# A fused retention and two-FFN kernel: early loads at once, w3 loaded ahead, integer adds in the weights' conversion, a separate pool for late raw words

## The chip, the cores and the metric

The kernel runs on one core of a Trainium2 chip. The metric is the device time of one execution in microseconds (us). TensorE is called PE here, VectorE DVE, ScalarE ACT, GpSimd POOL; SP is the engine whose queue issues most of the transfers.

## The reference, cut to what matters

```python
# attention: batch 4, heads 8, sequence 768, head size 64
for t in range(S):
    state = gamma[None, :, None, None] * state + np.einsum('bhd,bhe->bhde', k[:, :, t], v[:, :, t])
    y[:, :, t] = scale * np.einsum('bhd,bhde->bhe', q[:, :, t], state)
x = np.ascontiguousarray(attn_out.transpose(0, 2, 1, 3)).reshape(B * S, H * D)   # 3072 x 512
# first FFN: w_in 512 x 2048, w_out 2048 x 512
h = x @ w_in
g = np.where(h >= 1, h, np.where(h <= -1, 0.0, (h + 1) ** 2 / 4.0))
x = g @ w_out
# second FFN: w1, w2 512 x 1024, w3 1024 x 1024, w_out 1024 x 512
a = x @ w1
b = x @ w2
return ((a * b) @ w3) @ w_out
```

The inputs q, k and v are float32. The weights are drawn in float64, so each is a pair of 32-bit words in memory; the kernel makes a float32 of the pair on the chip.

## The kernel before, in words

**Retention** runs over 24 chunks of 128 tokens (six to a batch). A chunk `g` is three *pieces*: piece 0 multiplies kT and q (PE L348) and masks the result into `a_t` (DVE L391); piece 1 adds k and v to the state (PE L358, DVE L400 to L406); piece 2 makes the chunk's output (PE L372), whose high part is cast to `xh` (ACT L412) and whose rest is `xl` (DVE L417). Ahead of its pieces a chunk's q and v are scaled on POOL (`scale_chunk`, L315 and L316) into `q_t` and `vp`. q and kT have two buffers each, v and k one each. Four chunks make one tile of 512 tokens; six tiles share two buffers of `xh` and `xl`.

**First FFN.** A *slot* `n` is one tile and one of 16 blocks of 128 hidden features, 96 slots in all; `SLOTS` gives the order: features 0 to 7 of tile 0 (slots 0 to 7), then of tile 1, then 8 to 15 of both, then tiles 2 to 5 whole. A slot is 12 matmuls into `hps` (three passes over high and low halves, `mm3` at L102 to L104), the clipped square (ACT L461 and L462, DVE L463), and the product with `w_out` into `y1acc`: another 12 matmuls, or, for slots below `PLAIN`, 4 in plain float32 (L513).

**Conversion.** A weight pair goes through a *job*: raw words are loaded by SP (`load_job`, L127 and L131), ACT takes the absolute value of the high words (L168), and DVE shifts, masks and scales in five steps (L184 to L203), then adds the two parts (L215, L231 or L242). Early jobs hold 1024 words of each partition, later ones 512. `win` jobs and `wo` jobs alternate, and the raw words of all share two buffers, so that each kind has one. After slot `PLAIN` a second pool of conversion buffers takes the rest of `w_in` and `w_out`, and then the weights of the second FFN, which are converted and put back to memory (*spilled*). Between the steps of a job other work is set by a planner, which keeps estimates of when each engine is free (`now`) and lets a job's next step go if it fits in front of the next step of a slot.

**Second FFN.** w3 and the last weight are folded first: the *w3 stage*, 16 groups `u` of 12 matmuls into `w3acc`. Its w3 groups are fetched from memory (`fetch`, L275), each into one of two buffers, two groups ahead; in between the operands for the next stage are prepared. Then come 24 *units* into `bank_a`, `bank_b` and `bank_c` and the output products (`oacc`).

```python
def chunk_ahead(a):
    g, part = divmod(a, PIECES)
    if a < TILE_PIECES:
        if part == 0:
            if g:
                load_qk(g + 1)
            scale_chunk(g + 1)
        elif part == 1:
            load_k(g + 1)
            load_v(g + 2)
...
            load_w3(u + 1)
            if u + 2 < 2 * NF2:
                fetch(("w3", u + 2), spill[("w3", u + 2)])
            emit_w3o(u)
```

Of the kernel before, what the change touches and what calls it, by code (L numbers as in the profile page):

```python
# [16 lines left out]
P = 128  # L17
# [20 lines left out]
PLAIN = 11  # L38
SINGLE = 1
LATE = 5  # L40
# [9 lines left out]
def retention_then_two_ffns(  # L50
# [22 lines left out]
    ps_h = ctx.enter_context(tc.tile_pool(name="ps_h", bufs=2, space=bass.MemoryType.PSUM))  # L73
    ps_a = tc.tile_pool(name="ps_a", bufs=1, space=bass.MemoryType.PSUM)
    pairs_psum = ctx.enter_context(ExitStack())
    ps_a = pairs_psum.enter_context(ps_a)
    dram = ctx.enter_context(tc.tile_pool(name="dram", bufs=1, space=bass.MemoryType.DRAM))
    retention, splits, conversion = (ctx.enter_context(ExitStack()) for _ in range(3))
# [13 lines left out]
    state = const.tile([P, NP, D], F32, name="state")  # L92
    cpool = conversion.enter_context(tc.tile_pool(name="cpool0", bufs=2))
# [20 lines left out]

    def load_job(j):
        src, n, key, _ = j
        if key not in loaded:
            loaded.add(key)
            raw = cpool.tile([P, 2 * n], U32, tag="raw", name="raw")
            if key[0] == "win":  # L120
# [3 lines left out]
                for h in range(2):  # L124
                    for c in range(2):
                        for i in range(n // 512):
                            nc.sync.dma_start(  # L127
                                out=to[64 * c:64 * c + 64, i, h], in_=of[64 * h:64 * h + 64, i, :, c]
                            )
# [32 lines left out]
    magnitudes = {}  # L162

    def magnitude(job):
# [4 lines left out]
        magnitudes[key] = u  # L169
        now["conv"] = ready[("raw", key)] + 1.1  # L170

    def converter():

        while jobs:
            job = jobs.popleft()
            _, n, key, done = job
            if key not in magnitudes:
                magnitude(job)
            now["dve"] = max(now["dve"], now["conv"])
            raw, u = raws.pop(key), magnitudes.pop(key)  # L180
            lo, hi = raw[:, 0::2], raw[:, 1::2]
            w = cpool.tile([P, n], F32, tag="wf", name="w_f")
            uf, wu = u.bitcast(F32), w.bitcast(U32)
# [22 lines left out]
            yield 0.2 + n / 960  # L206
            if jobs:
                magnitude(jobs[0])
            if len(jobs) > 1:
                load_job(jobs[1])  # L210
            yield from done(w, uf)

    def done_win(f):
        def done(w, u):
            nc.vector.tensor_tensor(out=w, in0=w, in1=u, op=ALU.add)  # L215
# [10 lines left out]
    def done_wo(f):  # L226
        def done(w, u):
            for i in range(w.shape[-1] // 512):
# [11 lines left out]
    def done_spill(key):  # L240
        def done(w, u):
            nc.vector.tensor_tensor(out=w, in0=w, in1=u, op=ALU.add)  # L242
# [29 lines left out]
    def fetch(key, src):  # L272
        one = key[0] in ("wo2", "w3")
# [37 lines left out]
    def scale_chunk(g):  # L311
        if g >= NG:
# [4 lines left out]
            out=vp[g % 2],  # L317
# [16 lines left out]
    def piece_mm(a):  # L334
# [4 lines left out]
        q_t, kb, vb = ch[g], kp[g % 2], vp[g % 2]  # L339
        if part == 1 and c == NCH - 1:  # L340
            return
        ps = ps_a.tile([P, 2, 512], F32, tag="pa", name="pa")
        if part == 0:

            for p in range(NP):
                for h in range(2):
                    r = slice(64 * h, 64 * h + 64)
                    nc.tensor.matmul(  # L348
                        out=ps[:, h, p * C:(p + 1) * C], lhsT=kb[r, p, :], rhs=q_t[r, p, :],
# [3 lines left out]
        elif part == 1:  # L353

            for p in range(NP):
                for h in range(2):
# [3 lines left out]
                        lhsT=kt[g][:, d0:d0 + D], rhs=vb[:, 2 * p + h, :],  # L360
# [3 lines left out]
        else:  # L364


            for own in (False, True) if c else (True,):
                for j in range(NP // 2):
                    for h in range(2):
                        for e in range(2):  # L370
# [3 lines left out]
                                lhsT=vb[:, 2 * p + h, :] if own else sbd[r, p, :],  # L374
# [7 lines left out]
    def piece_ew(a):  # L382
# [6 lines left out]
        if part == 0:  # L389
            a_t = att.tile([P, 2, NP, C], F32, tag="a", name="a_t", bufs=1)  # L390
# [28 lines left out]
    def chunk_ahead(a):  # L419

        g, part = divmod(a, PIECES)
        if a < TILE_PIECES:
            if part == 0:
                if g:
                    load_qk(g + 1)
                scale_chunk(g + 1)
            elif part == 1:
                load_k(g + 1)
                load_v(g + 2)
        elif part == 0:  # L430
# [304 lines left out]
    with tc.manual_schedule():  # L735
# [6 lines left out]
        for at_, (kind, w, f, done) in enumerate(order):  # L742
# [7 lines left out]
        nc.sync.dma_start(out=decay, in_=c_decay)  # L750
        load_qk(0)
        load_v(0)
        nc.sync.dma_start(out=small, in_=c_small)
        scale_chunk(0)
        load_k(0)
        for h in range(2):
            r = slice(64 * h, 64 * h + 64)
            nc.sync.dma_start(out=block[r], in_=c_block[r, :, 64 * h:64 * h + 64])
        load_qk(1)
        now["dma"] = 9.0  # L760
        load_job(jobs[0])
        load_v(1)


        early = [jobs[1]]
        for a in range(TILE_PIECES):
            piece_mm(a)
            chunk_ahead(a)
            if a == 2:
                load_job(early.pop(0))  # L770
            piece_ew(a)
# [4 lines left out]
        for n in range(-1, NA):  # L776
# [11 lines left out]
            mine = [todo.popleft() for _ in range(mine) if todo]  # L788
# [211 lines left out]
```

## Time and profile before

| | us |
|---|---|
| median of three runs | 1108.78 (1108.28 to 1109.03) |
| profiled execution, whole | 1105.77 |
| its span (first to last instruction) | 1104.0 |
| PE busy | 1050.3 (95%), granted clock 0.985 of 2.4 GHz |
| DVE busy | 698.7 (63%) |
| ACT busy | 433.9 (39%) |
| POOL busy | 71.5 (6%) |
| moved by DMA | 166.03 MB, 150 GB/s on average |

The profiled execution is one run. The 1.77 us between its span and its whole time lie around the instructions, and it is 3.0 below the median.

### The profile page before, as it was taken

What the parts mean: (1) busy time and instruction counts of PE and PEld (TensorE: products, weight loads), DVE (VectorE), ACT (ScalarE), POOL (GpSimd) and SP (SyncE); (2) the same over time, 40 slices, a digit from 0 to 9 for tenths busy, and PEclk for the clock granted to TensorE, in tenths of its full rate; (3) what the DMA queues carried; (4) which work ended last, traced back from release to release, by engine and by line L of the source; (5) the groups of instructions that cost most, each with busy time, mean ns of one, the idle gap of its engine ahead of it and who ended that gap; (6) DMA issues with size and microseconds to landing.
All of it is one profiled execution on the core that took longest, in us unless ns stands there. A gap on an engine that the chain in (4) does not pass through costs nothing.

```text
span 1104.0 us, 14147 instructions
## 1 busy us (share of the span) xinstructions
PE 1050.3 (95%) x5444; PEld 828.7 (75%) x5444; DVE 698.7 (63%) x1130; ACT 433.9 (39%) x763; POOL 71.5 (6%) x67
## 2 busy tenths in 40 slices
PE   4789999899999999999999998689999999999998
PEld 3555578677777777777788886478888888888886
DVE  4798888688888878877835774553445334623340
ACT  1223355344444445454435664432333223412220
POOL 2212000011110100000000010000000000000000
PEclk9789999999999999999999999899999999999999
DMA  6545225254443544354303665554544345523412
GB/s 208 181 154 181 77 96 183 85 172 173 164 152 124 170 136 153 124 173 142 115 2 132 248 239 196 185 200 172 187 166 143 131 176 172 189 105 134 167 34 77
DMA packets 64116, 166.03 MB, mean 150 GB/s; under 512 B 7600, under 2 KB 15920, under 8 KB 59312
## 3 DMA queue, kind: packets, MB, share of 16 engines
q1 hardware_dynamic: 61744, 150.44, 40.1%
q0 software_dynamic: 2304, 14.68, 3.7%
q8 instruction: 43, 0.70, 0.2%
q14 instruction: 25, 0.20, 0.1%
HBM read 125.24 MB, written 39.85 MB: 150 GB/s over the span
## 4 chain that ended last, share of the span: by engine, by line
PE 84%; DVE 6%; DMA 5%; ACT 2%; SPq 1%; issue 1%; POOL 1%; ACTq 0%; POOLq 0%; DVEq 0%
PE bank_a L673 12%; PE hps L103 8%; PE y1acc L102 8%; PE hps L102 8%; PE hps L104 8%; PE y1acc L103 7%; PE y1acc L104 7%; PE bank_b L673 6%; PE oacc L718 4%; PE oacc L720 4%; PE oacc L719 4%; PE bank_c L673 3%; PE pa L372 3%; DMA f<-sp_w 2%; PE y1acc L513 2%; PE pa L348 2%
## 5 line engine op out<-in xcount | busy, mean ns | idle before, releaser
L102 PE MATMUL hps<-xh,win 128*128 128x512 f32 x384 | 154.7, 403 | 6.3 <-ACT win L98 5.0
L103 PE MATMUL hps<-xh,win 128*128 128x512 f32 x384 | 151.7, 395 | 0.5 <-DVE win L99 0.5
L104 PE MATMUL hps<-xl,win 128*128 128x512 f32 x384 | 150.8, 393 | 0.4 <-DVE xl L417 0.4
L673 PE MATMUL bank_a<-yop,unit 128*128 128x512 f32 x576 | 145.7, 389 | 0.0
L102 PE MATMUL y1acc<-gh,wo_s 128*128 128x512 f32 x340 | 139.0, 409 | 4.9 <-ACT wo_s L98 4.9
L461 ACT ACTIVATE r<-hps 128x512 f32<-128x512 f32 x96 | 57.3, 597 | 218.3 <-PE hps L104 218.3
L103 PE MATMUL y1acc<-gh,wo_s 128*128 128x512 f32 x340 | 134.2, 395 | 0.5 <-DVE wo_s L99 0.5
L104 PE MATMUL y1acc<-gl,wo_s 128*128 128x512 f32 x340 | 133.6, 393 | 0.0
L463 DVE SCALAR_TENSOR_TENSOR r<-hps,r 128x512 f32<-128x512 f32 x96 | 66.3, 691 | 101.2 <-ACT r L462 100.7
L673 PEld LDWEIGHTS bank_a<-yop,unit 128*128 128x128 f32 x576 | 108.1, 188 | 22.5
L699 DVE TENSOR_TENSOR c<-bank_b,c 128x512 f32<-128x512 f32 x24 | 16.6, 692 | 131.5 <-PE bank_b L673 131.5
L102 PEld LDWEIGHTS hps<-xh,win 128*128 128x128 f32 x384 | 72.6, 189 | 25.2 <-ACT win L98 5.7
L103 PEld LDWEIGHTS hps<-xh,win 128*128 128x128 f32 x384 | 72.6, 189 | 18.6 <-DVE win L99 1.6
L104 PEld LDWEIGHTS hps<-xl,win 128*128 128x128 f32 x384 | 72.7, 189 | 17.0 <-DVE xl L417 1.3
L102 PEld LDWEIGHTS y1acc<-gh,wo_s 128*128 128x128 f32 x340 | 64.1, 189 | 23.7 <-ACT wo_s L98 5.7
L104 PEld LDWEIGHTS y1acc<-gl,wo_s 128*128 128x128 f32 x340 | 64.1, 189 | 14.5
L103 PEld LDWEIGHTS y1acc<-gh,wo_s 128*128 128x128 f32 x340 | 64.2, 189 | 13.9 <-DVE wo_s L99 1.6
L474 ACT CAST gh<-r 128x512 fp32r<-128x512 f32 x85 | 52.9, 622 | 52.6 <-DVE r L463 52.6
L673 PE MATMUL bank_b<-yop,unit 128*128 128x512 f32 x288 | 73.1, 389 | 0.0
L475 DVE TENSOR_TENSOR gl<-r,gh 128x512 fp32r<-128x512 f32 x85 | 60.6, 713 | 14.9 <-ACT gh L474 13.8
L99 DVE TENSOR_TENSOR wo_s<-wo_f,wo_s 128x512 fp32r<-128x512 f32 x85 | 61.9, 728 | 1.9 <-ACT wo_s L98 1.9
L315 POOL TENSOR_TENSOR q_t<-q_t,decay 128x512 f32<-128x512 f32 x23 | 32.6, 1416 | 465.4 <-DMA q_t<-in_qT_dram 438.0
(152 smaller groups left out, 1716.6 us busy)
## 6 DMA issues: line engine op xcount, KB each, us to landing
unit<-wab_d SPq DMA_DIRECT2D x24, 1024.0 KB, 4.8
unit<-wab_d SPq DMA_DIRECT2D x24, 768.0 KB, 4.3
raw<-in_w_in_dram SPq DMA_DIRECT2D x64, 128.0 KB, 3.0
raw<-in_w_dram SPq DMA_DIRECT2D x16, 512.0 KB, 4.0
raw<-in_w3t_dram SPq DMA_DIRECT2D x16, 512.0 KB, 3.8
wab_d<-four POOLq DMA_DIRECT2D x8, 1024.0 KB, 5.2
raw<-in_w_out_dram SPq DMA_DIRECT2D x14, 512.0 KB, 3.6
q_t<-in_qT_dram SPq DMA_DIRECT2D x24, 256.0 KB, 4.4
```

The source lines that it names most:

```text
L99: nc.vector.tensor_tensor(out=lo, in0=src, in1=hi, op=ALU.subtract)
L102: nc.tensor.matmul(out=ps, lhsT=lh, rhs=rh, start=first, stop=False)
L103: nc.tensor.matmul(out=ps, lhsT=ll, rhs=rh, start=False, stop=False)
L104: nc.tensor.matmul(out=ps, lhsT=lh, rhs=rl, start=False, stop=last)
L461: nc.scalar.activation(out=r, in_=hps[n], func=AF.Relu, bias=0.5, scale=0.5)
L463: nc.vector.scalar_tensor_tensor(out=r, in0=hps.pop(n), scalar=1.0, in1=r, op0=ALU.max, op1=ALU.min)
L474: nc.scalar.copy(out=gh, in_=gs[n])
L475: nc.vector.tensor_tensor(out=gl, in0=gs[n], in1=gh, op=ALU.subtract)
L673: nc.tensor.matmul(out=ps, lhsT=x, rhs=z, start=first and kb + k == 0, stop=kb == 1 and k == 2, skip_group_check=True,)
L718: nc.tensor.matmul(out=ps, lhsT=lh, rhs=wh, start=(f == 0), stop=False)
L719: nc.tensor.matmul(out=ps, lhsT=lh, rhs=wl, start=False, stop=False)
L720: nc.tensor.matmul(out=ps, lhsT=ll, rhs=wh, start=False, stop=(f == NF2 - 1))
```

## The change

1. The sixteen loads of q, kT, v and k of the first four chunks go out at once on SP, into tiles of the pool that weights use later. The constants and the raw words of the first two `win` jobs go out on ACT's queue. The first tile's pieces follow a written order, `EARLY_ORDER`, with two PSUM buffers of their own.
2. A job's low words go through ACT (Relu with a scale, converted to integers), and DVE adds them as integers to the shifted and masked high words; the sign is joined in the step that writes to the destination. Per job DVE has two TENSOR_SCALAR, one integer add and one join per destination; before it had three TENSOR_SCALAR, two SCALAR_TENSOR_TENSOR and the adds.
3. `PLAIN` is 9, it was 11; `LATE`, the number of `win` and `wo` jobs that are cut in halves of 512, is 7, it was 5.
4. Raw words of late jobs have a pool of their own (`rpool`, two buffers), and the first two are loaded four slots before `PLAIN`.
5. w3 is fetched in the last eight slots, into eight tiles of two groups each (`fetch_w3`), not in the w3 stage.

```diff
-PLAIN = 11
+PLAIN = 9
+EARLY_ORDER = [(0, 0), (0, 1), (1, 0), (3, 0), (1, 1), (3, 1), (2, 0), (4, 0), (6, 0), (2, 1), (4, 1), (6, 1)]
+EARLY_ORDER += [(5, 0), (7, 0), (9, 0), (5, 1), (7, 1), (9, 1), (8, 0), (10, 0), (8, 1), (10, 1), (11, 0), (11, 1)]
-LATE = 5
+LATE = 7
...
-            raw = cpool.tile([P, 2 * n], U32, tag="raw", name="raw")
+            pool = rpool if key in late_keys else cpool
+            raw = pool.tile([P, 2 * n], U32, tag="raw", name="raw")
+            queue = nc.scalar if key in first_keys else nc.sync
...
+        r = cpool.tile([P, n], U32, tag="r", name="r")
+        nc.scalar.activation(out=r, in_=raws[key][:, 0::2], func=AF.Relu, scale=2.0 ** -29)
...
-            nc.vector.scalar_tensor_tensor(
-                out=wu, in0=hi, scalar=0xC0000000, in1=u,
-                op0=ALU.bitwise_and, op1=ALU.bitwise_or,
-            )
-            yield 0.2 + n / 960
-            nc.vector.tensor_scalar(
-                out=u, in0=wu, scalar1=0xFF800000, scalar2=None, op0=ALU.bitwise_and
-            )
-            yield 0.2 + n / 1920
-            nc.vector.scalar_tensor_tensor(
-                out=uf, in0=lo, scalar=2.0 ** -52, in1=uf, op0=ALU.mult, op1=ALU.mult
-            )
+            nc.vector.tensor_tensor(out=u, in0=u, in1=r, op=ALU.add)
...
+    def join(out, hi, u):
+        nc.vector.scalar_tensor_tensor(
+            out=out.bitcast(U32), in0=hi, scalar=0xC0000000, in1=u,
+            op0=ALU.bitwise_and, op1=ALU.bitwise_or,
+        )
...
-                nc.vector.tensor_tensor(
-                    out=t, in0=w[:, c0:c0 + 512], in1=u[:, c0:c0 + 512], op=ALU.add
-                )
+                join(t, hi[:, c0:c0 + 512], u[:, c0:c0 + 512])
...
+    def load_early():
+        for g in range(EARLY):
+            qk = wpool.tile([P, 2, 512], F32, tag="w", name="qk_e")
+            vk = wpool.tile([P, 2, 512], F32, tag="w", name="vk_e")
...
+            nc.sync.dma_start(out=ch[g], in_=qT[g])
+            nc.sync.dma_start(out=kb[g], in_=kT[g])
...
+            nc.sync.dma_start(out=vt[g], in_=v[g])
...
+            nc.sync.dma_start(out=kt[g], in_=k[g])
...
+    def fetch_w3(u):
+        t = late.tile([P, 2, 512], F32, tag="wc", name="w3f", bufs=NF2)
+        for i in range(2):
+            nc.sync.dma_start(out=t[:, i, :], in_=spill[("w3", u + i)])
+            arrived[("w3", u + i)] = t[:, i, :]
...
+        load_early()
         load_job(jobs[0])
-        load_v(1)
...
+        load_job(jobs[1])
+        load_qk(EARLY)
+        load_v(EARLY)
+        load_k(EARLY)
+        for g in range(EARLY + 1):
+            scale_chunk(g)
+        load_v(EARLY + 1)
+        for a, ew in EARLY_ORDER:
+            (piece_ew if ew else piece_mm)(a)
...
+            if n == PLAIN - 4:
+                for j in later[:2]:
+                    load_job(j)
...
+                if f >= NF2:
+                    fetch_w3(2 * (f - NF2))
...
-            if u + 2 < 2 * NF2:
-                fetch(("w3", u + 2), spill[("w3", u + 2)])
```

On SP, the loads from chunk 1 to the first `wo` job of before (`in_w_in` is a `win` job's raw words, `in_w_out` a `wo` job's):

```order
L291 DMA q_t<-in_qT_dram 128x512
L292 DMA kp_91<-in_kT_dram 128x512
L127 DMA raw<-in_w_in_dram 64x2x256 x4
L300 DMA v_t<-in_v_dram 128x512
L307 DMA k_t<-in_k_dram 128x512
L300 DMA v_t<-in_v_dram 128x512
L127 DMA raw<-in_w_in_dram 64x2x256 x4
L291 DMA q_t<-in_qT_dram 128x512
L292 DMA kp_90<-in_kT_dram 128x512
L307 DMA k_t<-in_k_dram 128x512
L300 DMA v_t<-in_v_dram 128x512
L131 DMA raw<-in_w_out_dram 128x2048
```

And in the changed program, from the loads of chunk 3 (`qk_e`, `vk_e`) on:

```order
L307 DMA qk_e<-in_qT_dram 128x512
L308 DMA qk_e<-in_kT_dram 128x512
L311 DMA vk_e<-in_v_dram 128x512
L313 DMA vk_e<-in_k_dram 128x512
L320 DMA q_t<-in_qT_dram 128x512
L321 DMA kp_87<-in_kT_dram 128x512
L329 DMA v_t<-in_v_dram 128x512
L337 DMA k_t<-in_k_dram 128x512
L329 DMA v_t<-in_v_dram 128x512
L141 DMA raw<-in_w_out_dram 128x2048
L320 DMA q_t<-in_qT_dram 128x512
L321 DMA kp_88<-in_kT_dram 128x512
```

The `win` loads are gone from this queue, and the first `wo` load stands behind all loads of chunks 0 to 4 and the second `v_t`, the v of chunk 5, which has the buffer of chunk 4's v.

On ACT, the rows around slots 0 and 1 of before (`u<-raw` is the absolute value, `r<-hps` and `r<-r` a slot's activation):

```order
L168 ACTIVATE u<-raw 128x1024
L461 ACTIVATE r<-hps 128x512
L462 ACTIVATE r<-r 128x512
L461 ACTIVATE r<-hps 128x512
L462 ACTIVATE r<-r 128x512
L168 ACTIVATE u<-raw 128x1024
L98 CAST win<-w_f 128x512 x2
```

And in the changed program:

```order
L179 ACTIVATE u<-raw 128x1024
L181 ACTIVATE r<-raw 128x1024
L490 ACTIVATE r<-hps 128x512
L491 ACTIVATE r<-r 128x512
L103 CAST win<-u 128x512
L179 ACTIVATE u<-raw 128x1024
L181 ACTIVATE r<-raw 128x1024
L490 ACTIVATE r<-hps 128x512
L491 ACTIVATE r<-r 128x512
```

A job now has two rows on ACT ahead of the slot's activation, the second (`r<-raw`) with the low words.

## Rows read from the trace of the kernel before

**Rows 1.** Windows by stage: length; busy us (instructions) of PE, PEld, DVE, ACT, POOL; clock, DMA share, GB/s.

```profile
0.00:42.98 42.98, 22.05 (x241) 17.97 (x241) 21.95 (x34) 7.20 (x11) 10.01 (x13) 0.84 0.66 207
42.98:114.90 71.92, 64.40 (x377) 39.63 (x377) 64.24 (x74) 24.25 (x34) 12.64 (x9) 0.95 0.47 154
...
204.00:224.00 20.00, 14.15 (x77) 10.46 (x76) 13.04 (x19) 6.38 (x11) 2.72 (x2) 0.91 0.31 102
224.00:674.26 450.26, 449.40 (x2574) 358.41 (x2572) 344.99 (x596) 220.15 (x396) 41.30 (x38) 1.00 0.44 150
674.26:739.87 65.61, 51.79 (x193) 38.98 (x194) 35.70 (x68) 25.88 (x52) 2.13 (x4) 0.92 0.64 227
739.87:1104.00 364.13, 359.80 (x1584) 296.80 (x1583) 146.71 (x227) 105.86 (x186) 0.00 (x0) 1.00 0.41 140
2.00:12.00 10.00, 4.93 (x48) 4.36 (x48) 2.34 (x3) 0.02 (x1) 2.30 (x2) 1.00 0.98 287
600.00:650.00 50.00, 50.00 (x223) 41.40 (x222) 39.12 (x87) 34.12 (x76) 5.51 (x10) 1.00 0.63 229
```

**Rows 2.** Timeline of PE, first matmuls of slots 0, 2, 8: start, us, [idle before, releaser].

```profile
42.98 0.50 PE L102 MATMUL hps<-xh,win 128*128 128x512 f32 x1 [0.69 <-ACT xh L412]
...
58.15 0.50 PE L102 MATMUL hps<-xh,win 128*128 128x512 f32 x1 [0.58 <-ACT win L98]
...
114.90 0.50 PE L102 MATMUL hps<-xh,win 128*128 128x512 f32 x1 [0.69 <-ACT xh L412]
```

**Rows 3.** The chain that ended last: start, us, engine and line.

```profile
118.67 3.43 PE y1acc L513 x8
...
187.42 1.09 PE pa L348 x16
...
200.56 1.62 PE pa L372 x32
...
207.73 0.59 ACT xh L412
...
212.65 0.62 ACT wo_s L98
...
684.58 6.61 DMA f<-sp_w
...
696.85 7.31 DMA f<-sp_w
...
748.02 2.72 PE bank_a L673 x12
```

**Rows 4.** Groups by shape: count, busy us, mean ns of one, idle before.

```profile
L194 DVE SCALAR_TENSOR_TENSOR w_f<-raw,u 128x1024 uint32<-128x1024 uint32 x10 | 12.2, 1225 | 0.3
L199 DVE TENSOR_SCALAR u<-w_f 128x1024 uint32<-128x1024 uint32 x10 | 6.9, 690 | 0.2
L231 DVE TENSOR_TENSOR wo_f<-w_f,u 128x512 f32<-128x512 f32 x16 | 14.4, 918 | 0.3
L391 DVE TENSOR_TENSOR a_t<-pa,small 128x1024 f32<-128x1024 f32 x24 | 29.2, 1215 | 4.6 <-PE pa L348 4.6
L463 DVE SCALAR_TENSOR_TENSOR r<-hps,r 128x512 f32<-128x512 f32 x96 | 66.3, 691 | 101.2 <-ACT r L462 100.7
L462 ACT ACTIVATE r<-r 128x512 f32<-128x512 f32 x96 | 60.6, 631 | 3.0
L168 ACT ACTIVATE u<-raw 128x1024 f32<-128x1024 f32 x10 | 11.5, 1155 | 9.5 <-DMA raw<-in_w_out_dram 6.8 <-DMA raw<-in_w_in_dram 1.7 <-DMA k_t<-in_k_dram 1.0
L316 POOL TENSOR_TENSOR vp<-v_t,small 128x512 f32<-128x512 f32 x24 | 30.9, 1288 | 8.0 <-DMA small<-in_c_small_dram 5.6 <-DMA v_t<-in_v_dram 2.4
```

**Rows 5.** DMA issues: KB each, median us from issue to landing.

```profile
raw<-in_w_out_dram SPq DMA_DIRECT2D x5, 1024.0 KB, 5.0
raw<-in_w_dram SPq DMA_DIRECT2D x16, 512.0 KB, 4.0
```

**Rows 6.** Waits of PE over the span: us, times, longest.

```profile
PE w3acc L102 <- ACT w3s L98: 10.9, 5, 5.0
```

More of the change, by code (lines that the diff above doesn't have):

```diff
@@ L72, in retention_then_two_ffns @@
     ps_acc = ctx.enter_context(tc.tile_pool(name="ps_acc", bufs=4, space=bass.MemoryType.PSUM))
[L73 to L76, printed above, removed]
+    early_psum, pairs_psum = (ctx.enter_context(ExitStack()) for _ in range(2))
+    ps_a = early_psum.enter_context(
+        tc.tile_pool(name="ps_e", bufs=2, space=bass.MemoryType.PSUM)
+    )
+    ps_h = None
     dram = ctx.enter_context(tc.tile_pool(name="dram", bufs=1, space=bass.MemoryType.DRAM))
[L78 removed]
+    retention, raw_late, splits, conversion = (ctx.enter_context(ExitStack()) for _ in range(4))
     const = retention.enter_context(tc.tile_pool(name="const", bufs=1))
@@ L113, in retention_then_two_ffns @@
     loaded = set()
+    late_keys = set()
+    first_keys = (("win", 0), ("win", 1))
     def load_job(j):
@@ L160, in dma, with tail @@
         return now["dma"] + 1.9
-    magnitudes = {}
-    def magnitude(job):
+    tails = {}
+    def tail(job):
         load_job(job)
@@ L176, in converter @@
             _, n, key, done = job
-            if key not in magnitudes:
-                magnitude(job)
+            if key not in tails:
+                tail(job)
             now["dve"] = max(now["dve"], now["conv"])
[L180 to L183, printed above, removed]
+            raw, (u, r) = raws.pop(key), tails.pop(key)
+            hi = raw[:, 1::2]
+            uf = u.bitcast(F32)
             nc.vector.tensor_scalar(
@@ L226, in done_wo, with done @@
     def done_wo(f):
-        def done(w, u):
-            for i in range(w.shape[-1] // 512):
+        def done(hi, u):
+            for i in range(u.shape[-1] // 512):
                 t = wpool.tile([P, 512], F32, tag="wo", name="wo_f")
                 c0 = i * 512
-                nc.vector.tensor_tensor(
-                    out=t, in0=w[:, c0:c0 + 512], in1=u[:, c0:c0 + 512], op=ALU.add
-                )
+                join(t, hi[:, c0:c0 + 512], u[:, c0:c0 + 512])
                 wo[f + i] = t
@@ L240, in done_spill, with done @@
     def done_spill(key):
-        def done(w, u):
-            nc.vector.tensor_tensor(out=w, in0=w, in1=u, op=ALU.add)
+        def done(hi, u):
+            w = cpool.tile([P, 512], F32, tag="wf", name="w_f", bufs=3)
+            join(w, hi, u)
             d = dram.tile([P, 512], F32, name=f"sp_{key[0]}_{key[1]}")
@@ L316, in scale_chunk @@
         nc.gpsimd.tensor_tensor(
-            out=vp[g % 2],
+            out=vb[g],
             in0=v_t,
@@ L338, in piece_mm @@
         c = g % NCH
-        q_t, kb, vb = ch[g], kp[g % 2], vp[g % 2]
+        q_t, k_, v_ = ch[g], kb[g], vb[g]
         if part == 1 and c == NCH - 1:
             return
-        ps = ps_a.tile([P, 2, 512], F32, tag="pa", name="pa")
+        if g < EARLY and part == 1:
+            ps = ps_acc.tile([P, 1, 512], F32, tag="acc", name="pa")
+        else:
+            ps = ps_a.tile([P, 2, 512], F32, tag="pa", name="pa")
         if part == 0:
@@ L389, in piece_ew @@
         if part == 0:
-            a_t = att.tile([P, 2, NP, C], F32, tag="a", name="a_t", bufs=1)
+            if g < EARLY:
+                a_t = wpool.tile([P, 2, 512], F32, tag="w", name="a_e")
+                a_t = a_t.rearrange("p h (a t) -> p h a t", a=NP)
+            else:
+                a_t = att.tile([P, 2, NP, C], F32, tag="a", name="a_t", bufs=1)
             nc.vector.tensor_tensor(
@@ L421, in chunk_ahead @@
         g, part = divmod(a, PIECES)
[L422 to L430, printed above, removed]
+        if part == 0:
             load_k(g)
@@ L748, in retention_then_two_ffns @@
                 (jobs if at_ < SINGLE else later).append(one)
[L750 to L755, printed above, removed]
+        late_keys.update(j[2] for j in later)
+        nc.scalar.dma_start(out=decay, in_=c_decay)
+        nc.scalar.dma_start(out=small, in_=c_small)
         for h in range(2):
             r = slice(64 * h, 64 * h + 64)
-            nc.sync.dma_start(out=block[r], in_=c_block[r, :, 64 * h:64 * h + 64])
-        load_qk(1)
-        now["dma"] = 9.0
+            nc.scalar.dma_start(out=block[r], in_=c_block[r, :, 64 * h:64 * h + 64])
+        load_early()
         load_job(jobs[0])
-        load_v(1)
[L765 to L771, printed above, removed]
+        load_job(jobs[1])
[7 more added lines that the diff above has]
+            (piece_ew if ew else piece_mm)(a)
+        early_psum.close()
+        ps_h = ctx.enter_context(tc.tile_pool(name="ps_h", bufs=2, space=bass.MemoryType.PSUM))
+        ps_a = pairs_psum.enter_context(
+            tc.tile_pool(name="ps_a", bufs=1, space=bass.MemoryType.PSUM)
+        )
         todo = deque(range(TILE_PIECES, NSTEP))
@@ L806, in retention_then_two_ffns @@
                     jobs.append((w3t[j][:, hf * 512:(hf + 1) * 512], 512, key, done_spill(key)))
+                late_keys.update(j[2] for j in jobs)
             for i in range(2):
```

44 lines of the change are left out of this document (27 added, 17 removed).

## Prediction

> **What bounds the kernel now.** The windows by stage come first [rows 1]. From 224 to 674 us PE is busy 449.40 of 450.26 us at clock 1.00, and from 739.87 to the end 359.80 of 364.13: TensorE bounds these 814 us, and no part of the change shortens a matmul there. The loss lies in four stretches. In 0 to 42.98, ahead of slot 0, PE works 22.05 us at a clock of 0.84; in 42.98 to 114.90, slots 0 to 7, it works 64.40 of 71.92; in 204 to 224 there is a hole, 14.15 busy of 20.00 at 0.91; and in the w3 stage, 674.26 to 739.87, it works 51.79 of 65.61 at 0.92. The first matmuls of slots 0, 2 and 8 on PE say what ended its wait [rows 2]: ScalarE's `win` or `xh` each time, that is a weight pair or x that came late. The chain [rows 3] names the links in the hole (`xh`, then `wo_s`) and in the w3 stage (`f<-sp_w`, a fetched w3 group). Last the groups by shape give the prices [rows 4], and the issues the time of a load [rows 5].
>
> **Term 1, start to slot 8: 42.98 and 71.92 now.** The first ten microseconds after 2 already move 287 GB/s at a DMA share of 0.98 [rows 1], so loading "at once" cannot go faster than that. New load ahead of slot 0: sixteen of 0.262 MB, 0.45 MB of constants, 1.05 MB of `win`: 5.70 MB, 19.8 us at that rate, so the last, k of chunk 3, lands near 21.8. Behind it stand the scaling of v(3) on POOL (1.29, [rows 4]), chunk 3's kv piece (about 0.6, bounded by the 1.09 of a qk piece) and out piece (1.62, [rows 3]), `xh` 0.59, and on VectorE state, one join, the second half of `win` and `xl`, about 0.6 each: slot 0 starts at 28 to 28.5 instead of 42.98.
>
> That does not carry over whole. The raw words of `wo` 0 are issued on SP behind v(5), whose single buffer waits for POOL's scaling of v(4). v(4) is three loads behind k(3), 24.4 at that rate, is scaled by 25.7, v(5) goes out, `wo` 0 is issued at 26.1 and lands 5.0 later [rows 5], at 31.1. Then ScalarE's Abs 1.16 and, new, Relu, which I price like Abs at 1.16 [rows 4]: 33.4. On ScalarE slot 0's two activations follow, 1.23, and a cast, 0.6; on VectorE their `r` 0.69, an `a_t` 1.22 and half of a `win`, 0.7: 37.3; then the job's own two shifts and masks (0.69 each), the add (1.4, below) and the first half's join 0.7: 40.8. The second half's join ends at 44.1, behind slot 1's `r`, whose matmuls end near 42 at the half clock; only this frees the raw buffer for the next `wo`: issued 44.1, landed 49.1, Abs and Relu to 51.4, and with a cast in between `hps` 2 starts near 52.6 (48 to 56), against 58.15 [rows 2]. Of 14.5 us gained at slot 0, 5.5 are left at slot 2.
>
> From there I count per two slots, since each pair converts one `win` and one `wo` job of 1024 words. Before: (114.90 − 58.15)/3 = 18.9, with VectorE busy 64.24 of 71.92 in this stretch, so about 16.9 of each 18.9; VectorE is what is short. Per job of 1024 words the last steps before are twice 1.225 (L194, and L203, which has its form), 0.69 (L199) and, on `wo`, two half adds of 0.918: 5.0. After, they are one integer add and two half joins, which are L194's form on 512 words, 0.7 each. The add runs on 16-bit halves, 128x2048 of them for 1024 words, a form that no row before has. Bounds: by bytes it is two fp32 rows of 512 words, and two-source rows on 512 words take 0.691 (L463): 1.4; by elements it is two rows of 1024 (L391, 1.215): 2.4. I take 1.4, since on the rows at hand the time goes with the bytes of a row, not with its type. So 2.8 for 5.0, 2.2 less per job, 4.4 per pair: VectorE falls from 16.9 to 12.5 per period (14.5 with the add at 2.4) and is no longer what bounds it.
>
> "VectorE: DVE Perf Modes" of the Trainium skill (the tier table) gives `tensor_tensor` on 16-bit data twice the rate of fp32; an estimate from it is 0.69 per 512 words, the lower bound again, and without that rate 1.2. No row here shows it yet.
>
> Two others are nearest then: PE itself, 2 × 2.72 + 2 × 3.43 + 3.3 for three pieces (1.09 and 1.62, and 0.6) = 15.6 [rows 3], and the ring of a `wo` raw buffer: load 5.0, Abs and Relu 2.3, shifts 1.4, add 1.4, joins 1.4, with slot work between them of 1.23 on ScalarE and 2.6 on VectorE: 15.3. So periods fall from 18.9 to about 16; the first is longer, 18.5, because PE comes back from its idle time at the half clock. Slot 8: 52.6 + 18.5 + 16.2 + 15.9 = 103.2 instead of 114.90. **Gain 11.7** (6 with the add at its upper bound, 1.0 in each of four ring passes, and `wo` 0 a microsecond or two later; 18 with `hps` 2 at 50 and no slow first period).
>
> "DMA: Bandwidth & Descriptors" of the Trainium skill (section on issuing engines) says that transfers issued by different engines run on the same 16 DMA engines, and only issue time is saved. By that the loads moved to ScalarE's queue come no earlier than I have them. Were the queues separate, 1.5 MB less would lie ahead of k(3): about 5 us more gain. The trace's 0.98 share at 287 GB/s speaks for the rule.
>
> **Term 2, PLAIN 11 to 9.** Two slots get twelve split matmuls (2.72) for four plain ones (3.43, [rows 3]): 2 × 0.71 = **1.4**. The split's cast and subtraction lie on ScalarE and VectorE, which are freer there.
>
> **Term 3, the hole at 204 to 224.** PE is idle 5.85 us of the 20 and loses about 1.6 more to the clock (0.91 of 2.4 GHz). The chain shows `xh` at 207.73 and `wo_s` at 212.65 [rows 3]: tile 2's first `xh` waits for a free x buffer until the last slot of tile 0 has read it, VectorE's `xl` stands right behind it, and behind that the conversion of a `wo`, for which `wo_s` is then late. In the changed program, all `wo` jobs stand ahead of that `xl` on VectorE; the wait for the buffer itself stays. I leave 1.4 us idle: **gain 6** (3 to 7).
>
> **Term 4, the w3 stage.** 65.61 long, 43.5 of it matmul. PE waits 10.9 us in five times for ScalarE's `w3s` [rows 6], and the chain puts fetches ahead of these: 6.61 and 7.31 us for 256 KB [rows 3], because a fetch needs one of two buffers, freed one group earlier. In the changed program w3 lies in SBUF before the stage, except where its buffers wait; so these waits go. What stays: start 1.7, the half clock after it 2, the sums of y about 1, and two waits at groups 9 and 10 for y, whose fetch is not moved, 0.7 and 3.4: 43.5 + 9 = 53. **Gain 11.5** (7 to 15). It adds 4.2 MB to slots whose DMA share is 0.63 already at 600 to 650 [rows 1], where PE has no idle time; I price that at nothing, since fetches there are for the stage behind, and keep a rival for it.
>
> Longer ScalarE work in late jobs (one Relu each, half of 1.16 for 512 words) lies under PE's 449 of 450 us: nothing, as ScalarE is busy 220 of 450 there.
>
> Sum: 11.7 + 1.4 + 6 + 11.5 = 30.6. Span 1104.0 − 30.6 = 1073.4, with 1.77 around it 1075.2 for a profiled execution. The median of before stands 3.0 above its profiled time; so **1078 us**.
>
> **Rivals.** (1) *The start's gain is kept whole*: if raw buffers are not the ring that I take them for, slot 0 at 28.5 carries on, slot 8 comes at 28.5 + 8 × 2.72 + 7 × 3.43 + 14 of pieces = 88, and the gain of term 1 is near 27; total 46, 1063. For it: VectorE was what was short. Against it: `wo` 0 lands at 31 whatever VectorE does. (2) *The later gains are given back*: fetches of w3, spilled words and y meet at 600 to 674, where 229 GB/s flow already, `wo` words or unit loads come late, or another link of the hole takes over; 15 to 18 in all, 1091 to 1094. (3) *Slower*: ScalarE, in order, now has two passes over the raw words, and each waits for a load (4.0 us for a 512 KB one, [rows 5]) that is issued only when the job two before is joined. With ScalarE held, the next slot's `r` and `gh` are late, and PE stands. There are 54 late jobs, so a stall of 30.6/54 = 0.57 us in each eats everything; at 1.1 us each it would be +59 − 30.6, near 1137. Against it: ScalarE is idle half the time at 224 to 674. The same sign comes if the add goes at some 5 us per 512 words. (4) *No change*: start and w3 stage both refilled by what is late next.
>
> **How the numbers follow.** The forecast has 65%, with its own range 1068 to 1091: all lower bounds together give 17.4, all upper ones 41.4; rival 1 15%, rival 2 12%, rival 3 5%, rival 4 3%. The range 1062 to 1094 takes in rivals 1 and 2 and leaves out 3, 4 and what lies beyond the bounds, under 2 in 10. About 0.2% (2.2 us) is what a measurement of this kernel can tell: faster 0.92, within it 0.03, slower 0.05.
>
> **What would show it.** Slot 0's first matmul near 28 and slot 2's near 52.6 with PE waiting for a `win` cast: right on the raw ring; slot 8 near 88 makes rival 1 right. The add's row at 0.7 per 512 words (1.4 per 1024) confirms its price. PE idle under 2 us in the stretch after tile 0's last slot: term 3. No wait of w3acc for `w3s` above 1 us, and PE's next stage 53 us after the last y1: term 4. Wrong if PE is not full from tile 2 to the w3 stage, or if idle time on ScalarE is ended by `raw` loads with PE waiting behind.

## The result, and the profile after

The changed kernel takes 1096.7 us (median of four runs, 1094.18 to 1099.98) where the kernel before, run beside it, takes 1108.9: ratio 0.9891, interval 0.9864 to 0.9919. It is faster by 12.2 us; 30.6 were forecast, and 1096.7 lies above the range of 1062 to 1094.

The windows of the changed kernel at the same events, columns as in [rows 1]: up to slot 0, slots 0 to 7, the stretch of the hole, up to slot 31, slots 31 to 58, the rest of the slots, the w3 stage.

```profile
0.00:32.82 32.82, 17.82 (x241) 15.41 (x241) 14.89 (x23) 6.38 (x10) 10.58 (x13) 0.94 0.81 228
32.82:110.34 77.52, 64.74 (x377) 40.25 (x377) 53.53 (x69) 33.32 (x45) 11.16 (x8) 0.94 0.48 161
...
197.00:217.00 20.00, 18.78 (x129) 14.60 (x128) 12.72 (x22) 8.95 (x17) 2.28 (x2) 1.00 0.42 132
217.00:262.00 45.00, 45.00 (x278) 35.44 (x276) 35.48 (x59) 24.14 (x42) 5.14 (x4) 1.00 0.58 193
262.00:444.00 182.00, 177.97 (x1064) 139.82 (x1064) 140.33 (x234) 102.42 (x177) 18.41 (x14) 0.99 0.60 190
444.00:674.46 230.46, 229.59 (x1234) 184.28 (x1233) 118.45 (x212) 112.27 (x212) 16.84 (x20) 1.00 0.32 113
674.46:730.00 55.54, 48.38 (x193) 38.29 (x194) 35.59 (x68) 25.91 (x52) 2.12 (x4) 0.94 0.57 205
```

PE is full in 217 to 262 and, but for 0.87 us, from 444 to the w3 stage. Between them it works 177.97 of 182.00 at a clock of 0.99, where before it was full. The w3 stage is 55.54 long instead of 65.61. PE's first matmuls of slots 0, 2 and 8, which answer to [rows 2]:

```profile
32.82 0.80 PE L107 MATMUL hps<-xh,win 128*128 128x512 f32 x1 [2.49 <-DVE xl L454]
...
55.98 0.80 PE L107 MATMUL hps<-xh,win 128*128 128x512 f32 x1 [6.18 <-ACT win L103]
...
110.34 0.50 PE L107 MATMUL hps<-xh,win 128*128 128x512 f32 x1 [0.68 <-ACT xh L449]
```

The gain can be followed slot by slot on ScalarE's first activation of each slot (`r<-hps`), which starts when the slot's first product is done and ScalarE has come to it; the last column is where PE starts the first unit. Times of before in us, then how much earlier (−) or later (+) each kernel is there. The runs other than "changed" are told below. Each row is one execution: e3 is the program of before up to the last eight slots, and yet some 3 us later from slot 0 on, so an entry by itself is good to about 3 us, and a change along a row to less.

| | slot 0 | slot 2 | slot 8 | slot 10 | slot 22 | slot 25 | slot 31 | slot 58 | slot 95 | first unit |
|---|---|---|---|---|---|---|---|---|---|---|
| before | 46.30 | 61.75 | 118.70 | 131.07 | 200.59 | 229.06 | 269.21 | 444.27 | 667.41 | 739.70 |
| changed | −8.96 | −0.25 | −5.05 | +0.48 | −0.38 | −7.00 | −6.99 | +0.20 | +0.21 | −9.86 |
| e1 | −8.27 | +1.03 | −4.38 | −1.23 | −1.67 | −8.34 | −8.34 | −8.22 | −8.22 | −18.14 |
| e2 | −8.61 | −7.31 | −11.23 | −7.80 | −6.60 | −13.28 | −13.24 | −11.54 | −11.53 | −23.27 |
| e3 | +3.06 | +2.10 | +3.10 | +3.07 | +3.07 | +3.05 | +3.05 | +3.05 | +3.05 | −7.25 |
| e5 | −10.13 | −1.76 | −4.07 | −3.43 | +1.76 | +2.38 | +2.38 | +2.38 | +2.38 | −10.95 |
| f1 | −7.68 | −6.38 | −10.85 | −8.98 | −9.71 | −16.39 | −16.39 | −16.39 | −16.39 | −29.34 |
| g2 | −8.47 | +0.68 | −1.59 | −1.62 | +4.15 | +3.06 | +3.07 | +3.06 | +3.07 | −8.55 |

So the changed kernel has its early gain of 5 us at slot 8, loses it at slots 9 and 10, gains 6.6 in the hole, loses 7.2 between slots 31 and 58, where PE was full before and nothing can be won back, and keeps only what the w3 stage brings, 10.1. What it loses at these two places it loses in one way. ScalarE's waits between slots 31 and 58 in the changed kernel (us, times, longest):

```profile
ACT u L179 <- DMA raw<-in_w3t_dram: 23.6, 11, 4.8
ACT u L179 <- DMA raw<-in_w_dram: 19.8, 9, 4.4
```

In the same window the kernel before has, for the raw words of w1 and w2, beside 0.4 us for `w_out` and nothing for w3:

```profile
ACT u L168 <- DMA raw<-in_w_dram: 1.0, 2, 0.7
```

And one turn of it in the chain of the changed kernel, slots 34 and 35:

```profile
287.77 0.68 DVE wo_s L104
288.45 0.61 DVE w_f L216
...
289.12 4.04 DMA raw<-in_w_dram
...
293.24 0.66 ACT u L179
293.90 0.55 ACT r L181
294.45 0.50 ACT r L490
...
294.97 0.64 ACT r L491
...
295.63 0.70 DVE r L492
```

The join at 288.45 (L216) frees a raw buffer; only then the next load goes out, 4.04 us long. ScalarE stands at the pass over these words (L179) until 293.24, does both passes, and only then comes to slot 35's activation (L490). That slot's `r` and its split, and PE behind them, are late. Of the 6.99 us that slot 31 was early, 2.09 are left at slot 35. At slots 9 and 10 the chain has the same with a `win` job, whose words hold up slot 9's split (`gh`), and PE behind it:

```profile
122.72 2.83 DMA raw<-in_w_in_dram
...
125.65 0.66 ACT u L179
126.31 0.55 ACT r L181
126.86 0.51 ACT gh L503
```

PE's first matmuls of slots 10 and 11 are 10.03 us apart there; before they were 6.17 apart:

```profile
122.65 0.79 PE L107 MATMUL hps<-xh,win 128*128 128x512 f32 x1
...
132.68 0.39 PE L107 MATMUL hps<-xh,win 128*128 128x512 f32 x1
```

The conversion's prices, groups by shape, which answer to [rows 4]:

```profile
L206 DVE CUSTOM_DVE_ANT_0 u<-u,r 128x1024 uint16<-128x1024 uint16 x56 | 38.6, 690 | 3.1
...
L179 ACT ACTIVATE u<-raw 128x512 f32<-128x512 f32 x56 | 37.8, 675 | 57.9 <-DMA raw<-in_w3t_dram 23.6 <-DMA raw<-in_w_dram 19.8 <-DMA raw<-in_w_in_dram 11.2
...
L181 ACT ACTIVATE r<-raw 128x512 uint32<-128x512 uint32 x56 | 37.0, 660 | 0.0
...
L206 DVE CUSTOM_DVE_ANT_0 u<-u,r 128x2048 uint16<-128x2048 uint16 x8 | 10.8, 1347 | 0.3
```

The add (L206) takes 0.690 us for 512 words: the lower bound. "VectorE: DVE Perf Modes" of the Trainium skill (the tier table), by which an estimate was 0.69, agrees with it; the row in the trace is a custom operation on 16-bit halves. Relu costs what Abs does (0.660, 0.675).

### The profile page after: what moved, and what is told of

Its sections match the earlier page's. It is cut to its first block, busy times and chain, and to the rows that moved or that the text cites. A ratio compares the mean times of both kernels' runs of the same rounds, so it can differ in the third digit from the quotient of the medians.

```text
span 1094.4 us, 14090 instructions
## 1 busy us (share of the span) xinstructions
PE 1045.9 (96%) x5452; PEld 828.2 (76%) x5452; DVE 620.1 (57%) x1017; ACT 473.5 (43%) x833; POOL 68.8 (6%) x67
## 4 chain that ended last, share of the span: by engine, by line
PE 68%; DMA 10%; DVE 10%; ACT 8%; SPq 2%; issue 2%; POOL 0%; ACTq 0%; DVEq 0%; POOLq 0%
PE bank_a L709 12%; PE bank_b L709 6%; PE y1acc L107 5%; PE y1acc L108 5%; PE y1acc L109 5%; PE hps L107 5%; PE hps L108 5%; PE hps L109 5%; PE oacc L754 4%; PE oacc L756 4%; PE oacc L755 4%; PE bank_c L709 3%; DMA raw<-in_w_dram 3%; DMA raw<-in_w3t_dram 2%; DMA raw<-in_w_in_dram 2%; ACT u L179 2%
## 5 line engine op out<-in xcount | busy, mean ns | idle before, releaser
L107 PE MATMUL y1acc<-gh,wo_s 128*128 128x512 f32 x348 | 142.8, 410 | 3.9 <-ACT wo_s L103 3.9
L108 PE MATMUL y1acc<-gh,wo_s 128*128 128x512 f32 x348 | 138.8, 399 | 4.1 <-DVE wo_s L104 3.9
L109 PE MATMUL y1acc<-gl,wo_s 128*128 128x512 f32 x348 | 137.5, 395 | 0.0
L490 ACT ACTIVATE r<-hps 128x512 f32<-128x512 f32 x96 | 56.8, 592 | 115.8 <-PE hps L109 115.6
L179 ACT ACTIVATE u<-raw 128x512 f32<-128x512 f32 (+1 forms) x64 | 46.9, 733 | 91.2 <-DMA raw<-in_w_out_dram 24.5
L107 PEld LDWEIGHTS y1acc<-gh,wo_s 128*128 128x128 f32 x348 | 65.8, 189 | 23.5 <-ACT wo_s L103 5.2
L108 PEld LDWEIGHTS y1acc<-gh,wo_s 128*128 128x128 f32 x348 | 66.0, 190 | 20.8 <-DVE wo_s L104 8.1
L709 PEld LDWEIGHTS bank_b<-yop,unit 128*128 128x128 f32 x288 | 54.1, 188 | 11.2
```

Of the source, the lines that this page charges most:

```text
L107: nc.tensor.matmul(out=ps, lhsT=lh, rhs=rh, start=first, stop=False)
L108: nc.tensor.matmul(out=ps, lhsT=ll, rhs=rh, start=False, stop=False)
L109: nc.tensor.matmul(out=ps, lhsT=lh, rhs=rl, start=False, stop=last)
L179: nc.scalar.activation(out=u.bitcast(F32), in_=raws[key][:, 1::2].bitcast(F32), func=AF.Abs)
L490: nc.scalar.activation(out=r, in_=hps[n], func=AF.Relu, bias=0.5, scale=0.5)
L709: nc.tensor.matmul(out=ps, lhsT=x, rhs=z, start=first and kb + k == 0, stop=kb == 1 and k == 2, skip_group_check=True,)
```

## The experiments

**The w3 part by itself (e3).** The kernel before, with w3 fetched as in the change:

```diff
-        one = key[0] in ("wo2", "w3")
+        one = key[0] == "wo2"
...
+                if f >= NF2:
+                    fetch_w3(2 * (f - NF2))
...
-            if u + 2 < 2 * NF2:
-                fetch(("w3", u + 2), spill[("w3", u + 2)])
```

> The kernel before with w3 fetched in the last eight slots and nothing else. If that part is worth by itself what the changed kernel's w3 stage shows (about 10 us less from the last slot to the first unit): 1098 to 1100 against 1108.9, ratio 0.991, and all the rest of the change gives 2 us. If the stage's gain needs the other parts, 1103 to 1109.

1097.03 us, ratio 0.9897 (0.9883 to 0.9912). This part alone gives 11.7 us, as much as the whole change. The loads, the integer add, PLAIN, LATE and the raw pool together give nothing measurable beside it: not because they are off the path, but because gains and losses cancel, as the table shows.

**The old steps in the changed kernel (e5).** One pass on ScalarE, five steps and an add on VectorE, all else as changed:

```diff
-        nc.scalar.activation(out=r, in_=raws[key][:, 0::2], func=AF.Relu, scale=2.0 ** -29)
...
-            nc.vector.tensor_tensor(out=u, in0=u, in1=r, op=ALU.add)
+            nc.vector.scalar_tensor_tensor(
+                out=wu, in0=hi, scalar=0xC0000000, in1=u,
+                op0=ALU.bitwise_and, op1=ALU.bitwise_or,
+            )
...
+            nc.vector.tensor_scalar(
+                out=u, in0=wu, scalar1=0xFF800000, scalar2=None, op0=ALU.bitwise_and
+            )
...
+            nc.vector.scalar_tensor_tensor(
+                out=uf, in0=lo, scalar=2.0 ** -52, in1=uf, op0=ALU.mult, op1=ALU.mult
+            )
...
```

> The changed kernel with the conversion's arithmetic of before: one pass on ScalarE, five steps and an add on VectorE; early loads, PLAIN, LATE, the raw pool and w3 ahead stay. Theory A: the raw words are free again before the next job's pass is written, and the job is longer, so loads are covered: no loss between slots 31 and 58, 7 us better there; the first slots slower, with periods of some 19 per two slots: 1088 to 1096. Rival: if the integer add is what saves time at the start and the loss in the middle has another cause, 1100 to 1106.

1096.89 us, ratio 0.9893 (0.9874 to 0.9913): the same time as the changed kernel, on another way. Nothing is lost between slots 31 and 58, as theory A has it, but the hole is not mended: slot 22 is 1.76 late, where the changed kernel is 7 early three slots on. By this run alone the integer add would seem to be worth nothing. It undoes the add, the second pass and the late last read of the raw words together, and so can't say which of them makes the loss.

**A third raw buffer for late jobs (e1).** One buffer more, used in turn; the order of instructions stays:

```diff
-            pool = rpool if key in late_keys else cpool
+            pool = cpool
+            if key in late_keys:
+                pool = third if turn[0] % 3 == 2 else rpool
+                turn[0] += 1
...
+                third = conversion.enter_context(tc.tile_pool(name="third", bufs=1))
```

> The changed kernel with a third buffer for the raw words of late jobs; nothing else moves. Theory A: ScalarE, in order, stands at a job's first pass until its raw words land (about 4 us), the load goes out only when the join of the job two before has freed the buffer, and slot work behind it on ScalarE is late for PE. Then ScalarE's waits for raw words between slots 31 and 58 (43 us in the changed kernel) fall under 10, the 7.2 us lost there come back, and part of the 5 us lost at slots 9 and 10: 1085 to 1090 us against 1096.7. Rival B: ScalarE's second pass as such is too much work ahead of the slots; then nothing moves, 1096 to 1098. Rival C: the DMA engines are what is late; then the loads take longer and nothing moves either.

1086.79 us, ratio 0.9798 (0.9782 to 0.9815), 9.9 us below the changed kernel. ScalarE's waits for raw words between slots 31 and 58 fall from 43.4 to 8.0:

```profile
ACT u L184 <- DMA raw<-in_w_dram: 5.6, 2, 2.8
ACT u L184 <- DMA raw<-in_w3t_dram: 2.4, 1, 2.4
```

Slot 31 is 8.34 early and slot 58 still 8.22. PE's first matmuls of slots 10 and 11 are 6.36 us apart:

```profile
123.32 0.79 PE L107 MATMUL hps<-xh,win 128*128 128x512 f32 x1
...
129.68 0.39 PE L107 MATMUL hps<-xh,win 128*128 128x512 f32 x1
```

The two passes are the same work as before (0.671 and 0.663 us here), so it is not the second pass as such (rival B), and the loads are the same loads (rival C).

**The passes behind the join (e2).** Two raw buffers as in the changed kernel, only the place of the passes is changed:

```diff
-            if jobs:
-                tail(jobs[0])
             if len(jobs) > 1:
                 load_job(jobs[1])
             yield from done(hi, u)
+            if jobs:
+                tail(jobs[0])
```

> The changed kernel with the two ScalarE passes of the next job put behind the join of the present one in the program, so that ScalarE reaches them later and the casts of a win pair stand ahead of them; two raw buffers as in the changed kernel. Theory A: the passes find their words landed, ScalarE is held less, PE loses less between slots 31 and 58: 1088 to 1092. Rival B: the same passes are only later, the weights come later by 1.2 us a job: 1097 to 1105.

1084.94 us, ratio 0.9782 (0.9767 to 0.9796), better than theory A's numbers. ScalarE's waits for raw words in the middle fall from 43.4 to 14.0, and slot 2 is 7.31 early instead of 0.25: there too it was ScalarE's wait for `wo` raw words, 6.90 us, that stood in front of the casts of `win` 2, which PE had waited 6.18 us for. Some of it is lost again between slots 8 and 22.

**Both (f1)**, the third buffer and the passes behind the join.

> The third raw buffer and the passes behind the join together. Theory A (ScalarE, in order, held by raw words that land late) has one cause behind both gains, so they don't add up: each alone took 10 and 12 us. What is left for the second: the 1.7 us that the moved passes still lose between slots 31 and 58, and part of the 4.6 us between slots 8 and 22: 1079 to 1084. If the two remedies mended different losses, 1075 or less.

1078.13 us, ratio 0.9728 (0.9709 to 0.9747): 18.6 below the changed kernel, where each alone gives 9.9 and 11.8. That is more than expected. The table says why: the two overlap between slots 31 and 58, where each alone brings back most of the 7.2; up to slot 8 the gain, 5.8, is that of the moved passes, since the third buffer, for late jobs only, doesn't reach there; and between slots 8 and 22 both bring back 3.5 where the buffer alone brings 2.0 and the moved passes nothing. The time is the forecast one, but that of another kernel and by other terms, so it confirms nothing of the sum. Of ScalarE's waits for raw words 2.3 us are left between slots 31 and 58, and PE is full there:

```profile
252.00:435.00 183.00, 183.00 (x1111) 144.99 (x1110) 146.01 (x238) 105.83 (x183) 18.35 (x14) 1.00 0.53 179
```

**The old steps in that kernel (g2).** The edit of the second run on top of both remedies, with the one pass behind the last add:

> The third raw buffer and the pass behind the join (1078.1 us with the integer add), with the conversion's arithmetic of before: prices the integer add where ScalarE is no longer held. Theory A: the two-pass conversion saves VectorE 2.2 us per 1024 words and pays off once its raw words are on time, in the first slots and in the hole at the first tile of 16 slots: 1084 to 1092. Rival: the arithmetic is worth nothing either way, as the changed kernel with the old steps was no slower: 1077 to 1080.

1097.01 us, ratio 0.9889 (0.9874 to 0.9903). The integer add, with Relu and the shorter job around it, is worth 18.9 us once ScalarE is not held, more than expected, and with the old steps the remedies are worth nothing (1097.0 and 1096.9). The rival fell. PE's longest sums of waiting for weights of the slots in this run (us, times, longest):

```profile
PE hps L107 <- ACT win L103: 11.5, 5, 3.7
...
PE y1acc L549 <- DVE wo_f L246: 4.1, 1, 4.1
PE y1acc L107 <- ACT wo_s L103: 4.0, 2, 3.5
```

These are weights that come late from VectorE, directly or behind ScalarE's cast: VectorE is busy 70.02 of 81.00 us from 33 to 114 here, where the changed kernel's is at 54.02.

**PLAIN and LATE.** The kernel with both remedies, at 11 and 5:

```diff
-PLAIN = 9
+PLAIN = 11
...
-LATE = 7
+LATE = 5
```

> Third raw buffer and passes behind the join, but PLAIN 11 and LATE 5 as in the kernel before. The prediction gave PLAIN 9 a gain of 1.4 us. By slots 9 to 22 of the runs so far it rather costs: pools change two slots earlier, with less converted ahead, and 3 to 5 us are lost between slots 9 and 22. If so, this is 1 to 4 us faster than with PLAIN 9; if the prediction's term holds, 1.4 slower.

1084.07 us, ratio 0.9777 (0.9753 to 0.98): 5.9 slower than at 9 and 7. The guess written with the run was wrong: the earlier change of pools is not what slots 9 to 22 lost. PE's first matmuls of slots 8 and 22 are 82.75 us apart before, 86.93 in the changed kernel, and 83.40 with both remedies at 9 and 7. Most of the 5.9 us lie ahead of slot 8: with 11 and 5 PE waits 4.22 us there for `xh`, with 9 and 7 0.68.

**Fewer issues for `win` raw words.** The raw tile's halves are laid out so that one transfer holds both features, first alone on the changed kernel:

```diff
-                        for i in range(n // 512):
-                            queue.dma_start(
-                                out=to[64 * c:64 * c + 64, i, h], in_=of[64 * h:64 * h + 64, i, :, c]
-                            )
+                        queue.dma_start(
+                            out=to[64 * c:64 * c + 64, h], in_=of[64 * h:64 * h + 64, :, :, c]
+                        )
...
```

The split then reads the new layout.

> The changed kernel with the win raw words in four transfers instead of eight and nothing else. If the win ring sets its first slots, the spacing of those loads on SP (16.9, 17.6, 17.7 us) falls by up to 2.5 us each and slot 8 comes 4 to 7 us earlier; the time falls by less, since ScalarE's waits for raw words behind slot 8 are still there and eat it by slot 58: 1093 to 1097. If issues go by rows, no change.

1097.01 us, ratio 0.9901 (0.9883 to 0.9919): no change. SP's rows of these loads in this run:

```profile
33.72 2.62 SPq L136 DMA_DIRECT2D raw<-in_w_in_dram  x4
...
51.20 2.50 SPq L136 DMA_DIRECT2D raw<-in_w_in_dram  x4
...
69.06 2.51 SPq L136 DMA_DIRECT2D raw<-in_w_in_dram  x4
...
87.15 2.51 SPq L136 DMA_DIRECT2D raw<-in_w_in_dram  x4
```

The same loads in the changed kernel:

```profile
34.61 5.25 SPq L137 DMA_DIRECT2D raw<-in_w_in_dram  x8
...
51.48 5.14 SPq L137 DMA_DIRECT2D raw<-in_w_in_dram  x8
...
69.11 5.15 SPq L137 DMA_DIRECT2D raw<-in_w_in_dram  x8
...
86.76 5.16 SPq L137 DMA_DIRECT2D raw<-in_w_in_dram  x8
```

Issue time halves, the spacing stays at 17 to 18 us. The theory that SP's issues set the period of the first slots fell. And on both remedies:

> The same with the raw words of a win job in four transfers instead of eight (two for a job of 512 words stay four): the halves' layout in the raw tile is changed so that one transfer holds both features. Theory on the first slots: the ring that sets the period there is that of the win raw words, whose eight issues alone keep SP 5.15 us, with 2.9 to land; with four issues SP needs 2.6 if the cost is by issue, and periods fall from 17 toward PE's 16: slot 8 some 3 to 6 us earlier, 1076 to 1081. If the cost of an issue is by rows moved, four take as long as eight, and nothing moves against the run before this one.

1077.99 us, ratio 0.973 (0.9708 to 0.9751), the same as without it.

**First raw words early.** On top of that, the raw words of the first two `win` jobs in the late jobs' pool, so that the next two loads find free buffers, and go out ahead of v of chunk 5:

```diff
+            if key in first_keys:
+                pool = rpool
...
+        load_job(jobs[2])
+        load_job(jobs[3])
         load_v(EARLY + 1)
```

> Third raw buffer, passes behind the join, win raw words in four transfers (1078.0 us), and the raw words of the first two win jobs in the late jobs' pool, so that the first wo and the next win load are free to go out right behind the loads of the first chunks and ahead of v of chunk 5. In the changed kernel the first wo load waited until 30.18 for the join of the first win job. If that load is what makes slots 1 and 2 late: wo raw words landed by 28 instead of 35, slot 2 some 4 to 8 us earlier, 1070 to 1075. If x and VectorE's order there are what is late, under 2 us: 1076 to 1079.

1076.6 us, ratio 0.9701 (0.9678 to 0.9723). The first `wo` load is issued at 20.17 instead of 29.10 in the run without it, slot 2 comes 3.0 us earlier and slot 8 2.3; of this 1.4 us are left in the median, less than its runs spread. That is the second expectation: the load was late, but not what decides.

**PLAIN 7, LATE 8** on the base of 1077.99:

```diff
-PLAIN = 9
+PLAIN = 7
...
-LATE = 7
+LATE = 8
```

> Third raw buffer, passes behind the join, win raw words in four transfers (1078.0 us), with PLAIN 7 and LATE 8. PLAIN 9 and LATE 7 were 6 us better than 11 and 5 in this company. If it goes on like that, two more split slots and the earlier change of pools: 1073 to 1077; if the first slots' conversion is then short of weights, 1080 or more.

1076.06 us, ratio 0.9709 (0.9691 to 0.9728): 1.9 better, about what the spread of its runs can tell.

**All together**, the early first raws and these two numbers.

> All of the run with the early first raws (1076.6 us) and PLAIN 7, LATE 8 (1076.1 alone on the same base of 1078.0). Both give up to the hole, where tile 2 waits for tile 0's x buffer and PE has slack no more: if their gains of 1.4 and 1.9 us add up, 1073 to 1075; if what one brings is lost again in front of the hole, 1075 to 1077.

1075.72 us, ratio 0.9713 (0.9686 to 0.974). The last two don't add up to more than either: 3.0% below the kernel before with the early first raws, 2.9% here, no difference that these runs can tell.

## Why the prediction was wrong, point by point

**The step that failed** is the one sentence "Longer ScalarE work in late jobs lies under PE's 449 of 450 us: nothing, as ScalarE is busy 220 of 450 there". ScalarE's time was priced by its busy share; what it cost was its waiting, in order, in front of slot work. That is the mechanism of rival 3, given 5%, and argued away with the same idle share. At 0.57 us for each of 54 late jobs it would have eaten the whole gain; between slots 31 and 58 it cost 7.2 us, 0.13 a job, of which PE stood 4.0 and the rest is work at a lower clock (0.99 against 1.00), and it cost 3.9 more from slot 10 to slot 11 (10.03 against 6.17). It didn't turn the sign, but it took some 11 us of the 18.4 that are missing. The third buffer alone (e1) brings back nearly all of the first and most of the second, and the moved passes (e2) most of the first. Together they reach 1078.13; 5.8 of their 18.6 us lie ahead of slot 8, in term 1.

What made the wait is in the code, and the prediction had both halves of it without joining them: in the old steps the raw words are last read before the next job's pass is written, so a load has the whole next job for cover, and that job was long. The new join reads the high words as the job's last step, behind the next job's passes, and a job of 512 words is some 1.1 us shorter on VectorE (an estimate from the means of its rows). The load is as long as ever, 4.0. This last account is argued from the code: no run takes the late last read and the shorter job apart.

**Term 1 (11.7) was oversized: 4.6** between slot 8's first matmul in [rows 2] and here, one execution each. Slot 0 came at 32.82 instead of 28.5. k of chunk 3 was issued at 17.78 and took some 5.9, landing near 23.7 and not 21.8, VectorE put the first `win` job's steps ahead of what x needed, and the first two of them took 0.85 and 1.15 beside POOL. Slot 2 came at 55.98 instead of 52.6: the first `wo` load waited until 30.18 not for v(5) but for the join of the first `win` job, whose raw buffer it takes, and the second, issued at 47.63 instead of 44.1, held ScalarE until 52.81. That is the chain that was forecast, some 3.5 us late. But it needs the two passes ahead of the casts, as the run with moved passes (e2) shows: its first `wo` load goes out no earlier, at 30.22, and slot 2 starts 5.2 us earlier:

```profile
50.81 0.49 PE L107 MATMUL hps<-xh,win 128*128 128x512 f32 x1 [1.20 <-ACT win L103]
```

Periods to slot 8 were 18.1, (110.34 − 55.98)/3, instead of about 16.9. With both remedies they are 17.6, (104.54 − 51.73)/3, so the held ScalarE explains a part only; SP's issues were ruled out, and what keeps them above PE's 15.6 stays open. No run undoes the early loads by themselves.

**Term 2 (1.4)** can't be seen in the changed kernel. With ScalarE free, PLAIN and LATE together give 5.9, so the sign was right, but the mechanism is not shown: most of it lies ahead of slot 8, where both settings run plain slots, and over the two slots that the term prices PE's first matmuls of slots 9 and 12 are 18.32 us apart with 9 and 7 and 18.53 with 11 and 5.

**Term 3 (6)** was right: 6.6 between slots 22 and 25. That the add pays for it, by having all `wo` jobs joined in time, is shown by the runs with the old steps: PE waits there for `wo_s`, 3.48 us at the longest in both, as it did before (3.02), and not at all in the changed kernel, and slot 25 is 2.4 and 3.1 late.

**Term 4 (11.5)** was right: 10.1 in the stage, 11.7 alone by medians. Rival 2 for it fell: PE is full up to the last slot.

**The add's price** was right, by a reason that its rows couldn't give: all of them have elements of 4 bytes, so bytes and elements can't be told apart there. VectorE's relief was right too: 53.53 of 77.52 us busy in slots 0 to 7, where it was 64.24 of 71.92. Rival 1 (the start's gain kept whole) fell with slot 2.

The Trainium skill's rule in "DMA: Bandwidth & Descriptors" (section on issuing engines) is in line with the trace: the loads on ScalarE's queue took 5.9 us each to land beside SP's loads of v and k, 5.6 and 5.9, and the stretch moved 228 GB/s at a share of 0.81. No run puts these loads back on SP.

## What to carry to other kernels

An engine that works in order and is half idle can still hold the engine that bounds the kernel: ask what it waits for in front of each urgent instruction, not how busy it is. When a change shortens a buffer's user or moves its last reader back, count the load again: the cover of a prefetch is the time from the last read to the next use. And a part that shows no gain when it is undone may be worth a lot: undone in the changed kernel the integer add made 0.2 us of difference, undone behind the remedies 18.9.

## What the runs showed of the hardware

Rows of VectorE whose sources lie in SBUF mostly took more than twice as long while POOL worked, those of two sources and those of one; a few, as one of `wo_s` at 499.30 with 0.68, did not. The join of 512 words (L216), twice in the changed kernel, and a TENSOR_SCALAR of 512 words (L201), which takes 0.42 to 0.43 in the 54 rows with POOL idle:

```profile
268.63 1.66 DVE L216 SCALAR_TENSOR_TENSOR w_f<-raw,u 128x512 uint32<-128x512 uint32 x1
...
288.37 0.69 DVE L216 SCALAR_TENSOR_TENSOR w_f<-raw,u 128x512 uint32<-128x512 uint32 x1
...
26.27 1.15 DVE L201 TENSOR_SCALAR u<-u 128x512 uint32<-128x512 uint32 x1
```

POOL at the time of the first; at the second it had nothing to do:

```profile
268.18 1.56 POOL L345 TENSOR_TENSOR q_t<-q_t,decay 128x512 f32<-128x512 f32 x1 [15.01 <-DMA q_t<-in_qT_dram]
269.70 1.49 POOL L346 TENSOR_TENSOR vp<-v_t,small 128x512 f32<-128x512 f32 x1
```

Rows that read a PSUM tile (`hps`, `pa`) took no longer: the seven of `r<-hps,r` that lay wholly beside POOL's rows took 0.68 to 0.69, as the other 89 did, and the six of `a_t<-pa,small` 1.21 to 1.22. One of the seven:

```profile
251.22 0.69 DVE L492 SCALAR_TENSOR_TENSOR r<-hps,r 128x512 f32<-128x512 f32 x1 [1.55 <-ACT r L491]
```

Transfers of the same raw words in four issues instead of eight cost SP half, 2.5 for 5.2 us, and took longer to land each, 4.8 for 3.0 us (medians). The last words of a job were there hardly earlier: by these figures 7.3 us after the first issue instead of 8.2.
